# Squares and norm sums of chunk 5's K issued ahead of chunk 2's first layer (delta-rule attention followed by a GELU feed-forward layer)

## The chip, the cores and the metric

One core of one Trainium2 chip runs the whole program. The metric is the device time of one execution in microseconds (us). Before the change it is 646.0 us, the median of three runs (645.03 to 646.12).

## The reference

Two blocks follow each other. The first is a delta-rule recurrence over 768 positions for 4 batches and 8 heads of width 48; the second is a two-layer feed-forward net with an exact GELU on 3072 tokens (width 384, inner width 2048). Everything is float32.

```python
k_n = k / (np.linalg.norm(k, axis=-1, keepdims=True) + 1e-06)
for t in range(S):
    y[:, :, t] = einsum('bhd,bhde->bhe', q[:, :, t], state)
    v_old = einsum('bhde,bhd->bhe', state, k_n[:, :, t])
    state = state + bt * einsum('bhd,bhe->bhde', k_n[:, :, t], v[:, :, t] - v_old)
x = y.transpose(0, 2, 1, 3).reshape(B * S, H * D)
h = x @ w_in
out = (0.5 * h * (1.0 + erf(h / sqrt(2)))) @ w_out
```

## The kernel before, in words

The 768 positions are cut into 12 chunks of 64. A chunk has two units (`tiles[c, a]`, a = 0, 1), each holding two batches on the 128 partitions. For a chunk the recurrence is solved in closed form: a matrix of products of the chunk's keys with each other (`grams`, L414/L425), scaled by beta over the squared norm of each key, is inverted by forward elimination (`eliminate_steps`, L475 to L517), and with the inverse come the updates (`solve`), the outputs (`use`) and the new state. The two chunks of a pair (2g and 2g+1) share one elimination: its 30 steps run on VectorE on all the pair's units at once. Then the chunk's output goes through the feed-forward net: its first layer (`part_of_layer`, matmuls at L916) in two halves of 11 products each, by a scheme that saves multiplications and adds sums on VectorE; its second layer (`second_layer`, matmuls at L859) in seven products.

The step the change moves is the preparation of the key norms of chunk 5. It has two parts:

- `norms(5)` (L335 to L345, through `squares`, L309 to L320): for each of the two units one ScalarE activation, Square, of the unit's key tile `Kn` (128x384) into a tile `ksq`. The tile comes from the pool tag "x", which has two buffers; the same two serve the units' output tiles `x` (written by VectorE at L758, read by the transposes at L788 or L779 that turn a chunk's output). The activations go through `keep`, whose helper line is L902.
- `prep(5)` (L347 to L351): for each unit one VectorE sum over the row (L349, 128x384 to 128x8) into a part of the tile `n`, and one GpSimd power (L351, exponent 0.5) on the 128x16 elements of `n` for both units together.

What follows from them is `finish(4)`: `factors` (L303, L305, L306, L307 on VectorE) turns the norms of chunks 4 and 5, one tile, into the scale `gm` of the pair, and the elimination's first step (`scales`, L476 and L477, then `flip`, L482, and `scaled_flip`, L487) consumes it. `n` of chunk 4 alone is also used by `scale_v` (L376 on GpSimd).

`Kn` of chunks 4 and up is loaded (L100, SyncE's queue) into two tiles Kp[2] and Kp[3] that all these chunks share: chunk 6's load can be issued only when chunk 5's squares have read the tiles.

The order of the work is a plan: a list of (time, step) pairs, sorted by time and then issued. The times are in units of a chunk's feed-forward stage: the layer products of chunk c lie between c + 1 and c + 2 for c >= 2, so chunk 2's first layer begins at 3.0. VectorE's queue keeps exactly this order. On ScalarE the steps made with `keep` keep their order among themselves; other instructions of ScalarE, and all of TensorE's, SyncE's and GpSimd's, are ordered by the scheduler that builds the program from the dependencies. The plan around the place of the change, as (time, step), is:

- 2.851 to 2.922: the last parts of chunk 2's attention: `outputs` (L748, L758) and `turns` (transposes, and the ScalarE copies `xT<-psX`, here at L780)
- 2.955: `turned_k` of chunk 5 (L399), 2.958: `mix_x` (L884, four sums of x), 2.96: `last_sum_of_w` (L846)
- 3.0 on: chunk 2's first layer, products P1, P5, P6, P2, R22, R11, P7, P3, R12, P4, R21. P6 has a VectorE sum behind it (L939, in place in PSUM tile psY, with `pu`), P7 another (L947, psY and `pu` into G), and P4 writes psY again, so it can start only when L947 has read psY. R12 is followed by L958.
- 3.06: `add_p5` (L968), and `norms(5)`, `prep(5)`
- 3.07: `sum_of_w(4)` (L842, 128x1536)
- 3.11: `finish(4)`; 3.112: `scales`; 3.16 on: `flip` and the elimination, in pieces up to 4.2.

In time order, the VectorE queue of that stretch reads L399, L884 (four), L846, L939, L968, L349 (two), L842, L303, L305, L306, L307, L476, L477, L947, L482, L487, L958, L496 and the elimination.

Of the kernel before, what the change touches and what calls it, by code (L numbers as in the profile page):

```python
# [19 lines left out]
def kernel(  # L20
# [617 lines left out]
    def join_steps(g):  # L638
        a, b = range(NA), range(NA, 2 * NA)
        return [(join_run, g, a, ()), (join_run, g, b, a), (join_run, g, (), b)]  # L640
# [413 lines left out]
    def at(first, last, steps):  # L1054

        total, done, timed = sum(s[0] for s in steps), 0.0, []
        for w, *step in steps:
            timed.append((first + (last - first) * (done + 0.5 * w) / total, step))
            done += w
        return timed  # L1060
# [128 lines left out]
    def state_at(c, *times, first=(), second=()):  # L1189

        steps = state_steps(c, first, second)
        if len(times) > len(steps):
            steps = steps[:-1] + [(turn, tiles[c, a]) for a in range(NA)]
        return [(t, step) for t, step in zip(times, steps) if t is not None]
# [45 lines left out]
    def gram(c):  # L1240
        return [(grams, [tiles[c, a] for a in range(NA)])] if c < NC else []

    def query(c):
        return [(queries, [tiles[c, a] for a in range(NA)])]

    def spread(name, n, *times):
        return [at(t, t + 0.001, [(1.0, copy_out, name, n)]) for t in times]

    def rows_of(g, w, pieces):
        rows = eliminate_steps(g)  # L1250
        assert sum(n for n, _, _ in pieces) == len(rows)
        parts, done = [], 0
        for n, first, last in pieces:
            parts += [at(w + first, w + last, rows[done:done + n])]
            done += n
        return parts
# [8 lines left out]
    for w in range(3, NC):  # L1265
        two_ahead = w + 2 < NC
        if w % 2:
            if w == 3:
                plan += [at(w + 0.19, w + 0.191, [(1.0, transposed, u, (1,)) for u in fourth]),
                         at(w + 0.1, w + 0.101, [(1.0, together, *gram(5))]),  # L1270
                         at(w + 0.06, w + 0.061, [(1.0, norms, 5), (1.0, prep, 5)]),
                         at(w + 0.11, w + 0.111, [(1.0, finish, 4)])]
                plan += rows_of(2, w, ((1, 0.112, 0.113), (2, 0.16, 0.2), (4, 0.224, 0.31),
                                       (2, 0.325, 0.365), (1, 0.395, 0.4), (2, 0.485, 0.5),
                                       (2, 0.508, 0.54), (5, 0.6, 0.685), (7, 0.76, 0.88),
                                       (3, 1.0, 1.05), (5, 1.07, 1.1), (1, 1.153, 1.154),
                                       (1, 1.2, 1.201), (1, 1.201, 1.202)))
            elif two_ahead:
                plan += rows_of(w // 2 + 1, w, ((1, -0.35, -0.349), (1, -0.34, -0.339),
                                                (1, -0.23, -0.229), (5, -0.22, -0.14),  # L1280
                                                (1, -0.07, -0.06), (3, 0.005, 0.05),
                                                (3, 0.068, 0.148), (2, 0.156, 0.215),
                                                (2, 0.235, 0.31), (3, 0.325, 0.365),
                                                (1, 0.398, 0.409), (2, 0.485, 0.5),
                                                (1, 0.508, 0.54), (5, 0.6, 0.685),
                                                (3, 0.76, 0.8), (1, 1.003, 1.004),
                                                (1, 1.16, 1.161), (1, 1.166, 1.167)))
            plan += [state_at(w, w + 0.367, w + 0.59, w + 0.72, w + 0.93, second=query(w))]
        else:
            j0, j1, j2 = join_steps(w // 2)  # L1290
            t = w + (0.25 if w == 4 else 0.165)
            plan += [at(t, t + 0.001, [(1.0, together, j0, *query(w))]),
                     at(w + 0.37, w + 0.371, [(1.0, together, j1, *gram(w + 2))]),
                     state_at(w, w + 0.465, w + 0.58, w + 0.72, w + 0.93, second=[j2] + gram(w + 3))]
            plan += spread("join", 4, w + 0.395)
            plan += spread("join", 4, w + 0.64)
            if two_ahead:
                plan += spread("gram", 2, w + 0.375) + spread("gram", 2, w + 0.42)
                plan += spread("gram", 4, w + 0.63)
                plan += [at(w + 0.366, w + 0.367, [(1.0, norms, w + 2)]), at(w + 0.3715, w + 0.372, [(1.0, prep, w + 2)]),  # L1300
                         at(w + 0.56, w + 0.561, [(1.0, norms, w + 3), (1.0, prep, w + 3)]),
                         at(w + 0.64, w + 0.641, [(1.0, finish, w + 2)])]
# [32 lines left out]
```

## Time and profile before

One profiled execution took 644.96 us by the clock of the device; the profile's span is 643.2 us, so 1.76 us lie around it.

| What | Value |
|---|---|
| median of three runs | 646.0 us |
| lowest, highest | 645.03, 646.12 us |
| the profiled execution | 644.96 us |
| its span | 643.2 us |
| TensorE matmul busy | 617.9 us (96%) |
| VectorE busy | 496.3 us (77%) |
| ScalarE busy | 259.9 us (40%) |
| GpSimd busy | 66.0 us (10%) |
| mean granted TensorE clock | 0.985 |
| TensorE matmuls | 9702 |

A profile here has several views. The page gives the busy share of each engine in 40 slices of the span (one slice is 16.08 us), each digit a tenth, and a row PEclk with the clock granted to TensorE in the same digits. The list of waits adds up, for each engine and line, how long the engine sat idle before instructions of that line and what released it. A timeline lists instructions in order: start in us from the span's start, total duration in us, engine, line, operation, output<-input, how many instructions are merged, and in brackets the idle time before them with its releaser. A table of windows gives the busy time of each engine in a stretch, with the granted clock. PE is TensorE, DVE VectorE, ACT ScalarE, POOL GpSimd, SP SyncE; L12 is line 12 of the kernel.

### The profile page before, as it was taken

Reading aid. Unit: us, or ns where it says so; the run is one execution under the profiler, and the core shown is the slowest. Engines: PE = TensorE matmul, PEld = TensorE weight load, DVE = VectorE, ACT = ScalarE, POOL = GpSimd, SP = SyncE. Lnnn points to the kernel's source line nnn. Section 1 sums busy time; section 2 is a strip of 40 time slices with the busy share of each in tenths; the row PEclk is TensorE's granted clock in tenths of the full one; section 3 lists DMA queues with packets and bytes.
Section 4 is the critical chain, followed back from the end, with each engine's and each line's share of the span. In section 5 each row is a group of like instructions: output and inputs, shape, how many; then the busy total and the mean of one; then the engine's idle time right before and its main releaser. Section 6 shows DMA issues by size and latency. Waiting matters only on the chain.

```text
span 643.2 us, 22156 instructions
## 1 busy us (share of the span) xinstructions
PE 617.9 (96%) x9702; PEld 573.8 (89%) x9702; DVE 496.3 (77%) x1011; ACT 259.9 (40%) x586; POOL 66.0 (10%) x58
## 2 busy tenths in 40 slices
PE   6759999999989999999999999999999999999997
PEld 5658876776879999999999999999999999999997
DVE  6999989989589997999577999577999565354342
ACT  4576767524632256132266132266132253132230
POOL 4044002001301003001003001013001000000000
PEclk9987999999989999999999999999999999999999
DMA  9794683204422335312325312411211400100100
GB/s 135 174 273 159 129 199 113 45 1 74 84 37 42 56 43 91 58 24 37 66 34 86 61 21 41 67 21 33 51 25 35 69 3 3 25 2 3 25 2 24
DMA packets 158433, 39.79 MB, mean 62 GB/s; under 512 B 150016, under 2 KB 153216, under 8 KB 158336
## 3 DMA queue, kind: packets, MB, share of 16 engines
q1 hardware_dynamic: 155664, 37.34, 30.0%
q10 hardware_dynamic: 2672, 1.03, 0.8%
q8 instruction: 76, 1.25, 0.8%
q14 instruction: 21, 0.17, 0.1%
HBM read 33.62 MB, written 4.72 MB: 60 GB/s over the span
## 4 chain that ended last, share of the span: by engine, by line
PE 77%; DVE 14%; DMA 2%; issue 2%; SPq 2%; ACT 1%; POOL 1%; DVEq 0%; POOLq 0%
PE psX L859 12%; PE psY L916 11%; PE psY L859 8%; PE psX L916 8%; PE psV L916 5%; PE psZ L916 5%; PE psZ L859 4%; PE psV L859 4%; PE psK L667 3%; DVE Nu L503 3%; DVE tmp L501 3%; PE psG L414 3%; PE psJ L593 3%; PE psH L811 2%; PE psY L732 2%
## 5 line engine op out<-in xcount | busy, mean ns | idle before, releaser
L916 PE MATMUL psX<-xT,w_in_sb 128*128 128x128 f32 x480 | 64.8, 278 | 0.0
L503 DVE TENSOR_TENSOR Nu<-Nu,tmp 128x58 f32<-128x58 f32 (+13 forms) x168 | 57.9, 344 | 5.8
L501 DVE TENSOR_TENSOR tmp<-Nu 128x58 f32<-128x58 f32 (+13 forms) x168 | 58.0, 345 | 4.4
L916 PEld LDWEIGHTS psX<-xT,w_in_sb 128*128 128x128 f32 x480 | 59.4, 193 | 0.9
L902 ACT COPY xT<-psX 128x768 f32<-128x768 f32 x9 | 7.2, 799 | 124.3 <-PE psX L788 124.3
L351 POOL TENSOR_TENSOR n<-n,half 128x16 f32<-128x16 f32 x10 | 31.4, 3145 | 251.8 <-DVE n L349 191.2
L859 PE MATMUL psX<-w_out_sb,G 128*128 128x192 f32 x320 | 55.3, 326 | 0.0
L859 PEld LDWEIGHTS psX<-w_out_sb,G 128*128 128x128 f32 x320 | 52.1, 190 | 0.0
L811 PE MATMUL psH<-xT,w_in_sb 128*128 128x256 f32 x192 | 45.2, 390 | 0.5 <-ACT G L902 0.4
L829 PE MATMUL psO<-w_out_sb,G 128*128 128x384 f32 x128 | 43.9, 490 | 0.0
L811 PEld LDWEIGHTS psH<-xT,w_in_sb 128*128 128x128 f32 x192 | 36.3, 193 | 8.0 <-ACT G L902 1.3
L916 PE MATMUL psY<-xT,w_in_sb 128*128 128x128 f32 x320 | 43.1, 279 | 0.0
L916 PEld LDWEIGHTS psY<-xT,w_in_sb 128*128 128x128 f32 x320 | 39.8, 196 | 0.0
L902 ACT COPY pu<-psZ 128x512 f32<-128x512 f32 x40 | 23.5, 587 | 39.3 <-PE psZ L916 37.7
L829 PEld LDWEIGHTS psO<-w_out_sb,G 128*128 128x128 f32 x128 | 23.6, 190 | 14.0
L902 ACT ACTIVATE G<-G 128x512 f32<-128x512 f32 x40 | 25.2, 630 | 23.3 <-DVE G L947 22.6
L939 DVE TENSOR_TENSOR psY<-psY,pu 128x512 f32<-128x512 f32 x20 | 14.0, 698 | 22.4 <-PE psY L916 19.6
L376 POOL TENSOR_TENSOR V<-V,n 128x384 f32<-128x384 f32 x18 | 17.0, 959 | 135.4 <-DMA V<-in_v_dram 115.5
L859 PE MATMUL psZ<-T,pu 128*128 128x192 f32 x160 | 28.6, 332 | 0.0
L859 PE MATMUL psY<-T,G 128*128 128x192 f32 x160 | 28.6, 332 | 0.0
L859 PE MATMUL psV<-w_out_sb,G 128*128 128x192 f32 x160 | 27.7, 326 | 0.0
L859 PE MATMUL psX<-T,G 128*128 128x192 f32 x160 | 27.6, 326 | 0.0
(183 smaller groups left out, 1346.1 us busy)
## 6 DMA issues: line engine op xcount, KB each, us to landing
Kp<-in_k_dram SPq DMA_DIRECT2D x76, 96.0 KB, 3.2
w_out_sb<-in_moe_w_in_dram SPq DMA_DIRECT2D x24, 256.0 KB, 4.1
w_raw<-in_moe_w_out_dram SPq DMA_DIRECT2D x16, 384.0 KB, 4.5
V<-in_v_dram SPq DMA_DIRECT2D x48, 96.0 KB, 3.1
out_dram<-o_sb SPq DMA_DIRECT2D x40, 96.0 KB, 2.2
Qp<-in_q_dram SPq DMA_DIRECT2D x64, 32.0 KB, 2.1
Qp<-in_q_dram SPq DMA_DIRECT2D x16, 96.0 KB, 4.7
Qp<-in_k_dram SPq DMA_DIRECT2D x32, 32.0 KB, 2.2
```

Of the source, the lines that this page charges most:

```text
L351: nc.gpsimd.tensor_tensor(flat, flat, half, op=ALU.pow)
L376: engine.tensor_tensor(u.V, u.V, ns[u.c][:, u.a].unsqueeze(2).to_broadcast([128, H, D]), op=ALU.mult)
L414: nc.tensor.matmul(psG[HALF[p], r, i * NP + j, :], lhsT=u.Kt[rows, p, j, :], rhs=(u.Qt if x else u.Kt)[rows, p, j, :], start=True, stop=True)
L501: nc.vector.tensor_tensor(tmp, nu[:, j + 1:, j:j + 1].to_broadcast([128, n, j]), nu[:, j:j + 1, 0:j].to_broadcast([128, n, j]), op=ALU.mult)
L503: nc.vector.tensor_tensor(nu[:, j + 1:, 0:j], nu[:, j + 1:, 0:j], tmp, op=ALU.add)
L593: nc.tensor.matmul(psJ[HALF[p], k, :], lhsT=(xm if level else off)[rows, us, :], rhs=zf[rows, us, HB:C] if level else xm[rows, us, :], sta ...
L667: nc.tensor.matmul(u.psK[to, x, r, j, :], lhsT=(u.Qt if x else u.Kt)[rows, p, j, :], rhs=St[rows, u.a, p ^ r, j, :], start=True, stop=True)
L811: nc.tensor.matmul(psH, lhsT=w_in_sb[:, f // 2, m, f % 2 * 128:(f % 2 + 1) * 128], rhs=xTs[c][:, m, :], start=(m == 0), stop=(m == NM - 1))
L829: nc.tensor.matmul(u.psO, lhsT=G[:, u.a, f, :], rhs=w_out_sb[:, f, :], start=(f == 0), stop=(f == NF - 1))
L859: nc.tensor.matmul(ps_, lhsT=lhs[:, f, :], rhs=rhs[:, f, :], start=first and f == 0, stop=f == FH - 1, skip_group_check=not first)
L902: i = fn(*args, **kw)
L916: nc.tensor.matmul(ps_[:, i], lhsT=lhs[:, f // 2, f % 2 * 128:(f % 2 + 1) * 128], rhs=rhs, start=first and i == 0, stop=True, skip_group_c ...
```

## The change

In the plan for w = 3, `norms(5)` moves from time 3.06 to 2.93 and `prep(5)` from 3.0605 to 2.961. Nothing else in the source is touched.

```diff
             if w == 3:
                 plan += [at(w + 0.19, w + 0.191, [(1.0, transposed, u, (1,)) for u in fourth]),
                          at(w + 0.1, w + 0.101, [(1.0, together, *gram(5))]),
-                         at(w + 0.06, w + 0.061, [(1.0, norms, 5), (1.0, prep, 5)]),
+                         at(w - 0.07, w - 0.069, [(1.0, norms, 5)]), at(w - 0.039, w - 0.038, [(1.0, prep, 5)]),
                          at(w + 0.11, w + 0.111, [(1.0, finish, 4)])]
```

In the built program the two Square activations on ScalarE stand behind the second copy `xT<-psX` (L780) and ahead of the copy `o_sb<-psO` (L833); before, they stood between the two groups of copies out of the gram tiles (L425). The two sums L349 on VectorE stand ahead of L939 and L968; before, behind them. The GpSimd queue and TensorE's are unchanged in order. Two small shifts come along: on ScalarE the GELU that follows L947 now stands ahead of both copies of chunk 3's turned queries (L394; before, between them), and on SyncE's queue the four loads of chunk 6's `Kn` stand ahead of one piece of a `Kb` load (L138) instead of behind it.

## The prediction

> **What bounds the kernel now.** I read the page's slices first: where TensorE is full and where its clock falls.
>
> ```profile
> PE   6759999999989999999999999999999999999997
> ...
> PEclk9987999999989999999999999999999999999999
> ```
>
> From slice 3 on TensorE is full, except in slice 11 (176.9 to 193 us): 8 in busy time and 8 in clock. The list of waits for 150 to 196 us says what it waited for there:
>
> ```profile
> PE psY L916 <- DVE G L947: 4.0, 1, 4.0
> DVE n L303 <- POOL n L351: 2.8, 1, 2.8
> ```
>
> One wait of 4.0 us: product P4, which writes psY again, waited for the sum L947 that reads it; and VectorE, two steps upstream, waited 2.8 us for the GpSimd power. VectorE's timeline shows why L947 was late (columns: start, duration):
>
> ```profile
> 168.60 0.70 DVE L939 TENSOR_TENSOR psY<-psY,pu 128x512 f32<-128x512 f32 x1 [2.77 <-ACT diag L425]
> 169.40 0.69 DVE L968 TENSOR_TENSOR pu<-psY,pu 128x512 f32<-128x512 f32 x1
> 170.40 1.01 DVE L349 TENSOR_REDUCE n<-ksq 128x8 f32<-128x384 f32 x2 [0.30 <-ACT ksq L902]
> 171.33 1.75 DVE L842 TENSOR_TENSOR T<-w_out_sb,T 128x1536 f32<-128x1536 f32 x1
> 175.87 0.18 DVE L303 TENSOR_SCALAR n<-n 128x32 f32<-128x32 f32 x1 [2.79 <-POOL n L351]
> ...
> 179.27 0.68 DVE L947 TENSOR_TENSOR G<-psY,pu 128x512 f32<-128x512 f32 x1
> ```
>
> L947 stands behind the six instructions of `finish(4)` and `scales` (L303 to L477), which wait for the norms. Its own data were long there: P7 ended at 173.35, the copy of pu at 173.63. The source of the chain is on ScalarE and GpSimd:
>
> ```profile
> 162.62 0.48 ACT L780 COPY xT<-psX 128x384 f32<-128x384 f32 x1 [0.64 <-PE psX L779]
> 164.56 0.48 ACT L833 COPY o_sb<-psO 128x384 f32<-128x384 f32 x1 [1.46 <-PE psO L829]
> ...
> 169.84 0.94 ACT L902 ACTIVATE ksq<-Kp 128x384 f32<-128x384 f32 x2
> ```
>
> ```profile
> 171.49 4.35 POOL L351 TENSOR_TENSOR n<-n,half 128x16 f32<-128x16 f32 x1 [10.76 <-DMA Kp<-in_k_dram]
> ```
>
> The bracket on the last line names a load, but in the program this power waits for VectorE only (the sums ended at 171.41); the load merely landed nearby. The table of windows prices the stall's second half, the clock after it:
>
> ```profile
> 176.00:180.00 4.00, 0.01 (x1) 0.00 (x0) 3.83 (x8) 0.01 (x1) 1.61 (x2) 1.00 0.38 46
> 180.00:185.00 5.00, 4.99 (x30) 4.99 (x31) 4.79 (x9) 2.02 (x4) 0.00 (x0) 0.66 0.32 38
> 185.00:190.00 5.00, 5.00 (x157) 4.88 (x155) 3.59 (x9) 2.06 (x5) 0.00 (x0) 1.00 0.02 5
> ```
>
> The column after POOL's is the granted clock: 0.66 for the five us after the gap, else 1.00. For the rest of the span, up to its last product, the list of waits names no other wait of TensorE, so what it gains here reaches the end, unless VectorE gives it back.
>
> **What the Trainium skill says.** "TensorE: Matmul & The Clock Gate", Part 1: the clock falls to half after an idle window of about 3.4 us and returns after about as long of sustained work. The trace agrees: a 4.0 us gap, then 0.65 (180 to 182), 0.50 (182 to 184), 0.99 (184 to 186). "GPSIMD Engine Reference", section 1, says the SBUF interfaces are shared with VectorE, with contention from instructions with two SBUF inputs. It agrees: of ten powers nine took 2.90 us, and the one that took 4.35 ran under L842, a sum of two SBUF tiles. "ScalarE: Activation LUTs", "What ACT_TABLE_LOAD costs", prices a switch of function set at 2.66 us; the squares stood between copies and took 0.94 us with no gap, and copies stand around them again, so I add none.
>
> **The change part by part.** Profiled times, in us.
>
> *Squares, 0.94 on ScalarE.* They move behind the copy `xT<-psX`, which ends at 163.10, and end at 164.04. The next copy, `o_sb`, waits for TensorE until 164.56 anyway. The cover is that idle 1.46; without it the copies of the first layer would slip by at most 0.94. Two conditions. The data: chunk 5's K is issued from 149.59 to 153.52 and lands in about 3.0 (at most 4.0), by 157.5. The buffers "x": chunk 2's turns read them last, at 162.6, before the copy ahead in the same queue. At the old place ScalarE gets 0.94 back, ahead of chunk 5's gram copies; nothing late waits for them. Zero.
>
> *Sums, 1.01 on VectorE.* They follow L846 (164.08, 1.75, end 165.83) and end about 166.8. VectorE then stood idle until 168.60 (2.77 idle), because P6's product ends only there; L939 does not move. Zero; with the cover gone at most 0.93, and P7 (172.29) would still not wait for L939's end at 169.3.
>
> *Power, 2.90 to 4.35 on GpSimd.* It starts about 166.85, between two SBUF-heavy sums, and ends at 169.75; with contention at 171.2. I take 2.90, though both are hidden: VectorE comes to L303 later than either.
>
> *What VectorE then does.* L968 at 169.40; the next start comes 0.61 after it (as at 187.28 to 187.89), so L842 at 170.01, end 171.76, L303 at 171.77 instead of 175.87: 4.10 earlier. Of these 2.8 are the wait on GpSimd, 1.3 the sums and their wait no longer in front of L842. L303 to L947 takes 3.40, so L947 starts at 175.17 and ends at 175.87.
>
> *TensorE.* P4 comes 0.06 after L947's end: 175.93, where TensorE's work ahead runs out at 175.84 to 176.0. So 180.01 minus 175.93 = 4.08 earlier, and no idle window. With it goes the cold clock: P4, R21 and the next P1 took 4.41 (180.01 to 184.42); at 0.893 for eight matmuls, as everywhere later, 2.68. That is 1.73 more. Sum 5.81.
>
> *What is late next.* VectorE is 4.10 ahead, TensorE 5.81: VectorE must catch up from idle time. It has 0.93 before L939 at 186.48 and 0.38 before L678 at 190.25, both on TensorE. With P6 ending at 180.5 and VectorE ready at 181.44, the first goes (lead 5.01); the second goes too (lead 5.39). Then VectorE has no gap until 237.09. So it falls 0.42 behind. Where it was more than 0.42 ahead of its reader nothing happens: L947 at 192.27 ends 0.8 before P4 at 193.77; chunk 3's outputs end 4.9 before the turns. The tight place is the start of chunk 3's first layer: the reads of the second layer's PSUM tiles (L1013 to L1018, end 218.40 to 219.31) and the sum T1 (L884, end 219.52) against products at 218.85 and 219.74. Slack 0.1 to 0.45, so TensorE loses 0 to 0.4 there: I take 0.3, far too short for the clock. After 237 VectorE has room. 5.81 minus 0.3 = 5.5.
>
> *Small moves.* The GELU after L947 now holds ScalarE's two copies of chunk 3's queries (L394) until about 176.5; they end by 177.7, and their readers (psK, 188.09 before, about 182.3 after) are not near. Chunk 6's four loads of K pass one Kb piece on SyncE: that piece slips about 2.7 us, and its reader runs at 242.56. `norms` and `prep` issue no DMA themselves. Zero.
>
> Against the profiled 644.96: 639.5. That execution lies 1.04 below the median and 0.07 below the lowest run; against the median of 646.0: **640.5**.
>
> **The rivals.**
> *The stall goes, but less is gained.* VectorE's queue is full from 180 to 237, and if its two gaps don't close, TensorE is held to VectorE's lead of 4.1: 641.9. The same comes out if another short gap leaves the clock cold. For it: VectorE busy 9 tenths in slices 12 to 14. Against: both gaps are waits on TensorE itself.
> *Nothing changes.* If the power's lateness is only the last of several, L947 keeps its place: 646. For it: L482 and the rest are queued together. Against: 2.79 of idle time ends with that power alone.
> *Slower: the squares block ScalarE's queue.* They now stand ahead of `o_sb`, both copies `pu` and chunk 4's gram copies. If K of chunk 5 landed late, at t, all of these would follow: `o_sb` and `pu` (1.1), L939, L968, L842 (3.1), then 3.4 to L947. It decides from squares ending at about 171.6, that is K landing after 170.7; each us beyond costs one, and 2 us late would give 648. Against: it lands by 157.5, 13 us of margin.
>
> **How the numbers follow.** Main case 0.76; less gained 0.17; no change 0.03; slower 0.02; the last 0.02 lies below the range. Main case alone: 5.2 to 5.9 less than 645.03 to 646.12, with no loss at chunk 3 at the far end. The range reaches from 645.03 minus 5.9 = 639.1 to 646.1 minus 4.1 = 642.0. About 0.2% (1.3 us) is what a measurement can tell from no change. Faster 0.95, same 0.03, slower 0.02.
>
> **What would show it.** ksq on ScalarE near 163.1; L349 near 165.8; the power near 166.9 and 2.9 long; L303 near 171.8 with no wait on GpSimd; P4 near 176 with at most 0.2 us of wait; clock 1.00 from 180 to 185; a short wait of TensorE on VectorE near 213, at chunk 3's first layer. Wrong would be: the squares held after 164.5, L303 still waiting, or the clock cold despite the closed gap.

## The result and the profile after

The changed kernel takes 640.36 us (median of three runs, 639.25 to 640.82) against 646.0: a ratio of 0.9908, 95% interval 0.9892 to 0.9924. Measured once more, beside other runs on one chip, it was 0.9909 (0.9894 to 0.9923; 639.86 against 646.06). The profiled execution took 640.36, with a span of 638.7.

On the page, slice 11 has lost its dip in busy time and clock:

```profile
PE   6779999999999999999999999999999999999997
...
PEclk9977999999999999999999999999999999999999
```

VectorE's timeline of the changed kernel (start, duration; idle time in brackets):

```profile
166.48 1.00 DVE L349 TENSOR_REDUCE n<-ksq 128x8 f32<-128x384 f32 x2
169.33 0.70 DVE L939 TENSOR_TENSOR psY<-psY,pu 128x512 f32<-128x512 f32 x1 [1.85 <-ACT diag L425]
170.13 0.69 DVE L968 TENSOR_TENSOR pu<-psY,pu 128x512 f32<-128x512 f32 x1
170.74 1.75 DVE L842 TENSOR_TENSOR T<-w_out_sb,T 128x1536 f32<-128x1536 f32 x1
172.41 0.17 DVE L303 TENSOR_SCALAR n<-n 128x32 f32<-128x32 f32 x1
...
175.80 0.68 DVE L947 TENSOR_TENSOR G<-psY,pu 128x512 f32<-128x512 f32 x1
```

The sums stand in idle time ahead of L939, and L303 has no bracket: nothing was waited for. This profile ran 0.73 late from before the place of the change (L939 at 169.33 against 168.60; it needs TensorE's P6 in both). I therefore compare starts minus the start of this L939 in the same profile. ScalarE and GpSimd, the source of the chain:

```profile
163.36 0.48 ACT L780 COPY xT<-psX 128x384 f32<-128x384 f32 x1 [0.64 <-PE psX L779]
163.73 0.94 ACT L902 ACTIVATE ksq<-Kp 128x384 f32<-128x384 f32 x2
165.29 0.48 ACT L833 COPY o_sb<-psO 128x384 f32<-128x384 f32 x1 [0.62 <-PE psO L829]
```

```profile
167.56 2.90 POOL L351 TENSOR_TENSOR n<-n,half 128x16 f32<-128x16 f32 x1 [6.09 <-DVE n L349]
```

The squares used up part of ScalarE's idle time before `o_sb` (0.62 of 1.46 is left); the power took 2.90 and ended at 170.46, 1.95 before L303. TensorE and the windows:

```profile
175.68 1.06 PE L916 MATMUL psV<-xT,w_in_sb 128*128 128x128 f32 x8
176.58 1.12 PE L916 MATMUL psY<-TX,w_in_sb 128*128 128x128 f32 x8
177.54 1.06 PE L916 MATMUL psY<-xT,w_in_sb 128*128 128x128 f32 x8
```

```profile
176.00:180.00 4.00, 4.00 (x38) 4.00 (x37) 3.96 (x4) 2.61 (x5) 0.00 (x0) 1.00 0.48 70
180.00:185.00 5.00, 5.00 (x156) 4.83 (x154) 4.59 (x15) 1.87 (x4) 0.00 (x0) 1.00 0.42 52
```

P4 (second line) follows R12 after 0.90, the usual distance of two groups of eight; the clock column is 1.00 throughout. Starts after L939, in us, from the timelines:

| Marker on TensorE | before | after | earlier by |
|---|---|---|---|
| P4 of chunk 2, first half | 11.41 | 7.25 | 4.16 |
| P6 of the second half | 16.71 | 10.89 | 5.82 |
| P2 of chunk 3's first layer | 52.93 | 47.52 | 5.41 |
| last product of the program | 467.77 | 462.45 | 5.32 |

### The profile page after: what moved, and what is told of

Read it like the earlier page. It is cut to its first block, busy times and chain, and to the rows that moved or that the text cites. A ratio compares the mean times of both kernels' runs of the same rounds, so it can differ in the third digit from the quotient of the medians.

```text
span 638.7 us, 22156 instructions
## 1 busy us (share of the span) xinstructions
PE 618.4 (97%) x9702; PEld 573.8 (90%) x9702; DVE 496.6 (78%) x1011; ACT 259.9 (41%) x586; POOL 64.9 (10%) x58
## 3 DMA queue, kind: packets, MB, share of 16 engines
q10 hardware_dynamic: 2672, 1.03, 0.8%
## 4 chain that ended last, share of the span: by engine, by line
PE 81%; DVE 11%; ACT 2%; DMA 2%; issue 2%; POOL 0%; SPq 0%; DVEq 0%; ACTq 0%; POOLq 0%
PE psX L859 12%; PE psY L916 11%; PE psX L916 8%; PE psY L859 8%; PE psV L916 5%; PE psZ L916 5%; PE psG L414 5%; PE psZ L859 4%; PE psV L859 4%; PE psK L667 3%; PE psO L829 3%; PE psJ L593 2%; DVE tmp L501 2%; DVE Nu L503 2%; PE psH L811 2%; PE psY L732 2%
## 5 line engine op out<-in xcount | busy, mean ns | idle before, releaser
L376 POOL TENSOR_TENSOR V<-V,n 128x384 f32<-128x384 f32 x18 | 17.2, 965 | 135.3 <-DMA V<-in_v_dram 131.1
L939 DVE TENSOR_TENSOR psY<-psY,pu 128x512 f32<-128x512 f32 x20 | 14.0, 699 | 20.5 <-PE psY L916 18.7
```

The lines of the kernel that those rows point to most:

```text
L376: engine.tensor_tensor(u.V, u.V, ns[u.c][:, u.a].unsqueeze(2).to_broadcast([128, H, D]), op=ALU.mult)
L939: nc.vector.tensor_tensor(L1["Y1"], L1["Y1"], L1["pu"][:, 0], op=ALU.add)
```

## The experiments

My theory: the gain is the wait of TensorE before P4 (about 4.1) and the cold clock after it (1.7), less what VectorE can't follow (0.3). It hangs on one thing, that the norms are ready when VectorE comes to L303. Rivals: the gain came from clearing ScalarE's queue; the slow products after the wait are no clock effect or hidden; earlier is simply better. The summary first; ratios are against the kernel before, the two middle columns are starts after L939 in each profile.

| Run | P4 | P6, second half | ratio (95% interval) |
|---|---|---|---|
| before | 11.41 | 16.71 | 1 |
| after, second measurement | 7.25 | 10.88 | 0.9909 (0.9894 to 0.9923) |
| e1 squares only | 11.02 | 17.39 | 0.9994 (0.9984 to 1.0004) |
| e2 L842 early | 9.97 | 15.27 | 0.9961 (0.9950 to 0.9971) |
| e3 one power more | 8.29 | 11.97 | 0.9927 (0.9912 to 0.9942) |
| e4 two powers more | 11.16 | 16.25 | 0.9994 (0.9983 to 1.0005) |
| e6 norms earlier | 7.25 | 10.89 | 0.9905 (0.9890 to 0.9919) |
| e7 wait filled, 7.1 us of matmuls | 14.39 | 17.97 | 1.0012 (1.0003 to 1.0020) |
| e8 wait filled, 3.7 us of matmuls | 11.40 | 15.08 | 0.9970 (0.9958 to 0.9982) |
| e10 squares and L842 early | 9.57 | 13.24 | 0.9960 (0.9946 to 0.9974) |
| e11 power and a quarter more | 10.09 | 15.12 | 0.9964 (0.9950 to 0.9977) |

**Which part of the move counts: the squares alone.**

```diff
-at(w + 0.06, w + 0.061, [(1.0, norms, 5), (1.0, prep, 5)]),
+at(w - 0.07, w - 0.069, [(1.0, norms, 5)]), at(w + 0.0605, w + 0.061, [(1.0, prep, 5)]),
```

> Only the two squares move (2.93); the sums and the power stay at 3.0605. My theory (the end of the power decides, and VectorE's order decides when it starts): the sums begin right after L968, 0.4 earlier than before; the power runs under L842 again and takes 4.35; L303 comes about 0.4 earlier; TensorE still waits about 3.6 before P4. If the clock goes cold all the same, 0.4 faster than before (ratio 0.999); if 3.6 is short enough to keep it warm, 2.1 faster (0.997). Rival (the gain came from clearing ScalarE's queue of the squares): nearly the whole 5.6, ratio 0.991.

Measured: P4 0.39 earlier, ratio 0.9994. The rival is out: ScalarE's queue was cleared exactly as in the changed kernel, and the times show no gain that can be told from none. The profile of this run:

```profile
170.78 1.75 DVE L842 TENSOR_TENSOR T<-w_out_sb,T 128x1536 f32<-128x1536 f32 x1
175.32 0.18 DVE L303 TENSOR_SCALAR n<-n 128x32 f32<-128x32 f32 x1 [2.79 <-POOL n L351]
```

```profile
170.95 4.35 POOL L351 TENSOR_TENSOR n<-n,half 128x16 f32<-128x16 f32 x1 [10.36 <-DVE n L349]
```

The sums come 0.4 earlier, but the power again starts under L842, takes 4.35, and VectorE waits 2.79 for it as before. P6 of the second half even comes 0.68 later than before, because the clock stayed low for longer after the wait; the section on the wait and the clock returns to this.

**Is it the readiness of the norms: making them late again in the changed kernel.** One or two more powers of the same size are put ahead of chunk 5's in GpSimd's queue; the four other queues keep their order.

```diff
-        nc.gpsimd.tensor_tensor(flat, flat, half, op=ALU.pow)
+        [nc.gpsimd.tensor_tensor(wk.tile([128, NA * H], F32, tag=f"late{i}", name="late", bufs=1),
+          flat, half, op=ALU.pow) for i in range(1 if c == 5 else 0)]
+        nc.gpsimd.tensor_tensor(flat, flat, half, op=ALU.pow)
```

> The changed kernel with one more GpSimd power of the same size ahead of chunk 5's, into a tile that nothing reads. My theory: the real power ends 2.9 later than in the changed kernel, 4.35 later if it meets L842; it had 1.9 to spare before L303. So L303 slips by 1.0 to 2.4, TensorE waits about that long before P4, the clock stays at 1.00, and the time is 1.0 to 2.4 over the changed kernel, still 3.2 to 4.6 below the kernel before (ratio 0.993 to 0.995). Rival (any wait of TensorE cools the clock): 1.7 more, 2.7 to 4.1 over the changed kernel.

The profile with one more, TensorE's timeline and then VectorE's:

```profile
178.10 1.16 PE L916 MATMUL psY<-TX,w_in_sb 128*128 128x128 f32 x8 [0.88 <-DVE G L947]
179.10 1.06 PE L916 MATMUL psY<-xT,w_in_sb 128*128 128x128 f32 x8
```

```profile
173.96 0.18 DVE L303 TENSOR_SCALAR n<-n 128x32 f32<-128x32 f32 x1 [0.99 <-POOL n L351]
```

L303 waits 0.99, P4 comes 1.04 later than in the changed kernel and P6 1.08: a wait of 0.88 costs itself and no clock. The ratio lies 0.0018 to 0.0019 over the changed kernel's two, which is 1.2 us.

> The changed kernel with two more such powers ahead of chunk 5's, into tiles that nothing reads. My theory: the real power ends 5.8 to 7.2 later, so L303 slips by 3.9 to 5.3; TensorE waits that long before P4, which is over the idle time that cooled the clock in the kernel before, and loses another 1.7 at the cold clock. 5.6 to 7.0 over the changed kernel: between the kernel before and 1.4 slower than it (ratio 1.000 to 1.002). Rival (the gain doesn't hang on when the norms are ready): it stays as fast as the changed kernel, ratio 0.991.

Two more (the same edit with 2) bring the old time back: ratio 0.9994. The wait before P4 is 3.74, and P4 to P6 takes 5.09 instead of 3.64, so 1.45 go to the clock. My upper end was too high, because the last power was not stretched by L842 (below). So the whole gain can be taken away on GpSimd alone.

**Earlier still.** Norms at 2.84 and prep at 2.85, ahead of chunk 2's state update.

```diff
-at(w - 0.07, w - 0.069, [(1.0, norms, 5)]), at(w - 0.039, w - 0.038, [(1.0, prep, 5)]),
+at(w - 0.16, w - 0.159, [(1.0, norms, 5)]), at(w - 0.15, w - 0.149, [(1.0, prep, 5)]),
```

> The changed kernel with norms and prep of chunk 5 moved earlier still, to 2.84 and 2.85, ahead of chunk 2's state update and outputs on VectorE. My theory (it only matters that the norms are ready before VectorE comes to L303; there were 1.9 to spare): the same time as the changed kernel, within 0.5. The squares now wait on ScalarE for chunk 4's sums to free their buffers and for chunk 5's K, until about 157.8, with nothing due behind them; VectorE waits about 1.5 for the sums before L748, and chunk 2's turns come at most 0.3 late. Rival (earlier is better): more gain. Rival (a place that blocks VectorE's queue costs what it blocks): 1.5 slower than the changed kernel.

The two markers of the table agree with the changed kernel's to 0.01, the last product to 0.05; the ratio is 0.9905. Both powers now run back to back from 158.73 and end eight us before they are read; it brings nothing. Being ready is enough.

**The clock by itself.** In the kernel before, TensorE's wait is filled with matmuls that nothing reads.

```diff
+            [behind(nc.tensor.matmul, t, block(1, 1)[:, 0, 0:128], of_x(c, 2, 0), True, True)
+             for t in ([dn("warm")[:, 0, 0:128]] * 32 if (c, b) == (2, 0) else [])]
             product(L1["Y1"], block(1, 1), L1["T"][4], False)
```

> The kernel before, with 32 matmuls (128x128 each, into a PSUM tile that nothing reads) put on TensorE between R12 and P4, where it waits for L947. They take 3.6 of the 4.0, so P4 starts where it did. My theory (the second part of the gain is the cold clock): the clock stays at 1.00 from 180 to 185, P4, R21 and P1 take 2.7 instead of 4.4, and the kernel is 1.7 faster than before although it does more work and waits as long: 644.2, ratio 0.9973. Rival (the slow products after the wait come from something else, or their slowness is hidden): 646, no change.

I had mis-sized it. One such matmul counts as two pieces of 0.11, so 32 took 7.1 us and P4 came 2.98 later than before. Even so P6 came only 1.26 later and the time rose by 0.0012 (0.8 us): 1.72 came back at a warm clock. With half as many:

> The kernel before with 16 instead of 32 matmuls (128x128, read by nothing) between R12 and P4: the profile of the 32 showed 64 pieces and 7.1 us, so 16 take 3.6, which fit into the wait of 4.0. My theory (the second part of the gain is the cold clock): clock 1.00 after the gap, P4 starts where it did, and the eight-matmul groups after it take 0.89 from the first on; 1.7 faster than before, 644.3, ratio 0.9973. Rival (the slow groups are something else than the idle time's clock): 646, no change.

Measured 0.9970, 644.20 against 645.91. The timeline of TensorE and the windows of this run:

```profile
175.55 3.74 PE L892 MATMUL warm<-xT,w_in_sb 128*128 128x128 f32 x32
179.71 1.16 PE L916 MATMUL psY<-TX,w_in_sb 128*128 128x128 f32 x8 [0.42 <-DVE G L947]
180.71 1.06 PE L916 MATMUL psY<-xT,w_in_sb 128*128 128x128 f32 x8
```

```profile
178.00:180.00 2.00, 1.58 (x14) 1.39 (x13) 2.00 (x3) 0.31 (x1) 0.00 (x0) 1.00 0.43 50
180.00:182.00 2.00, 2.00 (x20) 2.00 (x20) 1.97 (x2) 1.00 (x3) 0.00 (x0) 1.00 0.43 52
```

P4 starts where it did in the kernel before (11.40 against 11.41), the clock stays at 1.00, and P6 comes 1.63 earlier. The kernel does more and waits for the same sum, and is 1.7 us faster: the cold clock is the second part of the gain, shown apart from the first. The seven executions lie within 0.7 us of each other, those of the kernel before on the same chip within 3.0, which fits a loss to the clock that differs from one execution to the next.

**The contention between the power and L842.** The kernel before with L842 in VectorE's idle time.

```diff
-at(3.07, 3.071, [(1.0, sum_of_w, 4)])
+at(2.962, 2.963, [(1.0, sum_of_w, 4)])
```

> The kernel before, with L842 (the sum of second-layer weights, 128x1536) moved from 3.07 to 2.962, into VectorE's idle time ahead of L939. Norms stay late. My theory: the power no longer runs under a sum of two SBUF tiles and takes 2.90 instead of 4.35, so L303 and L947 come about 1.5 earlier and TensorE waits about 2.5 instead of 4.0. If the cold clock needs an idle time of more than about 3.4, it stays warm and the gain is 1.5 + 1.7 = 3.2 (ratio 0.995); if any wait of some us brings it, the gain is 1.5 (0.9977). Rival (the power is slow for another reason, its place in time or the loads in flight): 4.35 again, no gain.

```profile
172.75 2.90 POOL L351 TENSOR_TENSOR n<-n,half 128x16 f32<-128x16 f32 x1 [10.76 <-DMA Kp<-in_k_dram]
```

```profile
179.82 1.16 PE L916 MATMUL psY<-TX,w_in_sb 128*128 128x128 f32 x8 [2.56 <-DVE G L947]
180.82 1.47 PE L916 MATMUL psY<-xT,w_in_sb 128*128 128x128 f32 x8
182.07 1.92 PE L916 MATMUL psX<-xT,w_in_sb 128*128 128x128 f32 x8
```

The power takes 2.90, P4 comes 1.44 earlier. But in this profile the wait of 2.56 is followed by slow groups (1.47, 1.92 where 1.06 is normal): P4 to P6 takes 5.30, as in the kernel before. So the limit of 3.4 us that the prediction had taken over failed here. The ratio, 0.9961 or 2.5 us, lies between the two values I had named, and its sixteen executions show why: eight took 642.61 to 642.94, about 3.3 below the kernel before, which is the value for a warm clock; the other eight, the profiled one among them, took 643.58 to 645.86.

**How long a wait cools the clock.** Both edits e1 and e2 at once, and the changed kernel with one power and a small one more (16 and 4 columns).

> The kernel before with both the squares at 2.93 and L842 at 2.962; the sums and the power stay at 3.0605. My theory: the sums follow L968 at once, the power takes 2.90 with nothing under it, L303 comes 1.9 earlier than before, and TensorE waits about 2.1. The wait of 2.56 in the run with L842 early still cooled the clock and one of 0.88 didn't; if 2.1 is enough for it, the gain is 1.9 (ratio 0.997), if not, 1.9 + 1.7 = 3.6 (0.9944).

> The changed kernel with two more GpSimd powers ahead of chunk 5's, one of 16 columns and one of 4, into tiles that nothing reads. If the time of a power goes with its columns, the small one takes about 0.7 and TensorE waits about 1.6 before P4; if it is the same for any size, 2.9 and 3.8. With 1.6 and a warm clock, 1.6 over the changed kernel (ratio 0.9935); with 1.6 and a cold one, 3.3 over it (0.996); with 3.8, as with two full powers (0.9994).

```diff
+        [nc.gpsimd.tensor_tensor(wk.tile([128, w], F32, tag=f"late{w}", name="late", bufs=1),
+          flat[:, 0:w], half[:, 0:w], op=ALU.pow) for w in ((16, 4) if c == 5 else ())]
         nc.gpsimd.tensor_tensor(flat, flat, half, op=ALU.pow)
```

P4 of the first run, then of the second:

```profile
178.36 1.16 PE L916 MATMUL psY<-TX,w_in_sb 128*128 128x128 f32 x8 [2.16 <-DVE G L947]
179.35 1.06 PE L916 MATMUL psY<-xT,w_in_sb 128*128 128x128 f32 x8
```

```profile
179.81 2.08 PE L916 MATMUL psY<-TX,w_in_sb 128*128 128x128 f32 x8 [2.68 <-DVE G L947]
181.67 1.55 PE L916 MATMUL psY<-xT,w_in_sb 128*128 128x128 f32 x8
```

After 2.16 the groups are at full speed (P4 to P6 3.67), after 2.68 not (5.03). The ratio of e10, 0.9960 or 2.6 us, lies between my two values, and its eight executions fall into two groups: three at 642.10 to 642.59, the profiled one among them, and five at 643.75 to 644.33. The groups lie 1.7 apart, the size of the clock's loss. So I read that a wait of about 2.2, like that of 2.56 in e2, cools the clock in some executions and not in others; the five were not profiled, so this is not shown directly.

In e11 the small power took 1.01 where I had expected 0.7. The real power started only 0.5 later than in e3, but that was 0.32 behind the start of L842, and it was stretched to 4.19; so the wait was 2.68 and not 1.6.

What decides it can be read from the clock column in narrow windows. e2, where the clock fell after P4 had started:

```profile
180.00:182.00 2.00, 2.00 (x16) 2.00 (x17) 1.97 (x2) 1.39 (x3) 0.00 (x0) 0.82 0.40 49
182.00:184.00 2.00, 2.00 (x12) 2.00 (x11) 1.93 (x5) 0.60 (x1) 0.00 (x0) 0.50 0.39 45
184.00:186.00 2.00, 2.00 (x16) 2.00 (x16) 1.25 (x5) 1.26 (x3) 0.00 (x0) 0.82 0.25 30
```

In windows of 0.25 us the clock is either 1.00 or 0.50, except at the two ends. So a mean of 0.82 over 2 us means 0.7 us at 0.50, and the clock was low from about 181.3 to 184.7. The same reading of all the profiles with a longer wait:

| Profile | TensorE waits | clock at 0.50 | half of that after P4's start | measured loss, P4 to P6 |
|---|---|---|---|---|
| before | 176.01 to 180.01 | 180.61 to 184.02 | 1.71 | 1.66 |
| e1 | 175.87 to 179.47 | 178.33 to 185.15 | 2.84 | 2.73 |
| e4 | 176.29 to 180.03 | 179.61 to 183.02 | 1.50 | 1.45 |
| e2 | 177.26 to 179.82 | 181.30 to 184.71 | 1.71 | 1.66 |
| e11 | 177.13 to 179.81 | 179.28 to 182.70 | 1.44 | 1.39 |
| e10 | 176.20 to 178.36 | never | 0 | 0.03 |

The low stretch lasts 3.41 us, once twice that, and what it costs is half of the part that falls on work. Its ends are not tied to the wait: in a profile the changes of the clock lie whole multiples of 3.413 apart (before: up at 57.73 near the program's start, down at 180.61, 36 multiples later, up again one later). If each profile is cut into stretches of that length, TensorE was idle for 1.9 us or more (1.9 to 3.3) in the stretch that ended with each of the five falls, and for at most 1.5 in every stretch around the wait after which the clock stayed up. In e10 a boundary, counted on from the clock's changes near the start, fell into the wait and left 1.5 before it and 0.6 behind. That is a reading of these profiles, not a run of its own; it explains why the same wait can cost 1.7 in one execution and nothing in another.

**Where 0.4 to 0.5 of the gain went.** The changed kernel with VectorE's turns of chunk 4's queries moved out of the tight place at chunk 3's first layer.

```diff
-        t = c + (-0.12 if c % 2 == 0 else 0.23)
+        t = c + (0.16 if c == 4 else -0.12 if c % 2 == 0 else 0.23)
         plan += [at(t, t + 0.01, [(1.0, turned_q, u) for u in us])]
```

> The changed kernel with the two turns of chunk 4's queries on VectorE (L404, 1.23 together) moved from 3.88, ahead of the reads of the second layer's PSUM tiles, to 4.16, behind L512. My theory (what is lost between the gain of 5.8 at chunk 3's state products and 5.3 at the end is VectorE being late at chunk 3's first layer): the reads L1013 to L1018 and the sums L884 come 1.2 earlier against TensorE, the two short waits at that layer's first products go, and 0.3 to 0.5 more is gained: 640.0, or 0.4 below the changed kernel, best seen in the profile at those products. Rival (the rest was lost elsewhere, or is noise between runs): no change there, the same time.

In this kernel the load of chunk 5's queries comes ahead of the turns of chunk 4's, so chunk 4 computes with the wrong queries; the instructions and their sizes are the same. The time did not improve (0.9915, 0.9901 to 0.9930). The first products did come earlier (P2 of chunk 3 at 47.10 after L939 instead of 47.52), but the list of waits names a new one:

```profile
PE psY L916 <- ACT G L902: 0.9, 1, 0.9
```

The turns now delay L516, and ScalarE's copies L520, which wait for it, stood ahead of the GELU that frees psY. The second try mends both: the load of chunk 5's queries goes from 4.1 to 4.18, and the copies L520 from 4.201 to 4.26, so that they stand behind that GELU.

```diff
+        t = 3.2 if c == 4 else c - (0.72 if c % 2 == 0 else 0.82 if c == 5 else 0.9)
...
-                                       (1, 1.2, 1.201), (1, 1.201, 1.202)))
+                                       (1, 1.2, 1.201), (1, 1.260, 1.261)))
```

> The changed kernel with the turns of chunk 4's queries (L404) at 4.16 as before, the load of chunk 5's queries behind them, and the last elimination step (the copies L520 on ScalarE) moved from 4.201 to 4.26, so that the GELU of psY stands ahead of them. My theory: the 0.3 to 0.5 that TensorE lost at chunk 3's first layer stays won, since the wait of 0.9 for that GELU, which ate it in the first try, goes: 0.4 below the changed kernel, ratio 0.990, seen in the profile as no wait of TensorE and the second psX group of chunk 3's first layer 0.4 earlier. Rival: another wait takes its place, the same time as the changed kernel.

Chunk 3's first two products in the changed kernel, then in this one:

```profile
213.94 1.13 PE L916 MATMUL psX<-xT,w_in_sb 128*128 128x128 f32 x8
214.97 1.16 PE L916 MATMUL psZ<-TX,Sw 128*128 128x128 f32 x8
```

```profile
213.21 1.05 PE L916 MATMUL psX<-xT,w_in_sb 128*128 128x128 f32 x8
214.10 1.06 PE L916 MATMUL psZ<-TX,Sw 128*128 128x128 f32 x8
```

The distance of the two is 1.03 in the first and 0.89, the usual, in the second. P2 stands at 47.11, the last product at 461.96 against 462.45: 0.5 us more, which shows where VectorE's lateness reached TensorE. (In e10's profile the first of these products waits 0.15 for L1013 by name.) It is the fastest kernel here, 639.32 us (639.19 to 639.50), ratio 0.9894 (0.9879 to 0.9910), but the intervals overlap with the changed kernel's: that it is faster is shown by the profile's markers, not by the times.

Why VectorE was late there shows further up. Compared as before by starts after L939, it is ahead of the kernel before by 5.18 at the second half's L939 and by 5.82 at L684 and L958, as far as TensorE; 3 us later, and from there on to chunk 3, by 5.33. In between, two of its short instructions were longer (they take 0.34 to 0.38 otherwise), each while GpSimd ran a product of V (L376):

```profile
189.66 0.83 POOL L376 TENSOR_TENSOR V<-V,n 128x384 f32<-128x384 f32 x1 [15.32 <-DMA V<-in_v_dram]
190.89 0.87 POOL L376 TENSOR_TENSOR V<-V,n 128x384 f32<-128x384 f32 x1 [0.41 <-DMA V<-in_v_dram]
```

```profile
189.83 0.86 DVE L501 TENSOR_TENSOR tmp<-Nu 128x184 f32<-128x184 f32 x1
191.11 0.87 DVE L501 TENSOR_TENSOR tmp<-Nu 128x198 f32<-128x198 f32 x1
```

In the kernel before only one was:

```profile
196.11 0.88 DVE L503 TENSOR_TENSOR Nu<-Nu,tmp 128x198 f32<-128x198 f32 x1
```

One such instruction more is the 0.5. The profiles of the second measurement and of e3, e5, e6, e9 and e10 have two as well. No run moved L376, so that it could be won back there is not shown.

## Why the prediction was right

640.5 was forecast, 640.36 measured, and the main steps hold one by one: the wait before P4 goes, and the cold clock with it. That the median came within 0.14 is luck: the changed kernel's executions lie up to 1.6 us apart, and the second measurement gives a gain of 6.2 where the first gives 5.6.

- *Squares, sums, power.* All three stood where the working put them, within 0.1 once the 0.73 is taken off, and hid behind the covers named. The squares alone moved P4 by 0.39 (e1).
- *L303 and P4.* 4.10 was forecast for L303; it came at 3.08 after L939 instead of 7.27, so 4.19. P4: forecast 4.08, measured 4.16.
- *The clock.* 1.73 forecast, 1.66 measured between P4 and P6, and 1.7 in a run of its own (e8). The price was read from one execution, and that it fits the median is partly luck: e1's profile lost 2.73 after a shorter wait.
- *VectorE late at chunk 3.* The place was right, the reason wasn't. 0.3 was forecast out of 0 to 0.4; 0.41 was measured between P6 and P2, and another 0.1 by the end. It surfaced where the prediction said and was won back there by moving 1.2 us of VectorE work (e9). But VectorE was to be 0.42 behind because its idle time would not suffice to catch up. It caught up fully, to 5.82, and then lost 0.49 to GpSimd's products of V, which the prediction doesn't name. That the two come to about the same is luck.
- *The slower rival.* The squares found their data in time: 0.62 of idle time was left before `o_sb`. A late load of K was not tried.

Two more reasons were less right than the number. I took over the limit of the Trainium skill, "TensorE: Matmul & The Clock Gate", Part 1, an idle window of about 3.4 us, and wrote that the trace agrees; 4.0 couldn't test it. The length of 3.4 us does come back here, as that of the low stretches. But waits of 2.56 and 2.68 cooled the clock in the profiled executions, 0.88 and 2.16 didn't, and by the spread of the executions 2.2 and 2.56 do it in some and not in others. The measurement decides. For this change it made no difference, since the wait goes altogether; for half the change it would have.

The other is the stretched power. The Trainium skill, "GPSIMD Engine Reference", section 1, names contention with VectorE instructions that have two SBUF inputs, and I read "ran under L842". The count behind it was also wrong: of the ten powers seven took 2.90, one 2.94, one 3.85 (the first, at 51.42) and the one in question 4.35. In e3 the real power ran from 171.02 to 173.92, almost wholly under L842 (171.22 to 172.97), and took 2.90. What counts is the start:

```profile
171.02 2.90 POOL L351 TENSOR_TENSOR n<-n,half 128x16 f32<-128x16 f32 x1
```

It began 0.20 before L842. In the five profiles where it began 0.16 to 0.32 after L842's start it took 4.19 to 4.35, and ended 2.75 to 2.77 after L842's end each time. So it looks as if it waits for the running sum to finish and is not slowed by it. The first power of the program, which I didn't take apart, need not follow the same count.

## What to carry to other kernels

When a full engine waits once, walk back to the first instruction whose inputs were ready long before, and move that into idle time ahead; being ready in time is all that counts, and going earlier brings nothing. Price the wait with what the clock costs after it, here 1.4 to 2.7 us in the profiles where a wait of 2.6 us or more was followed by a low clock, and measure more than one execution, since the same wait may cost it or not. Then ask who falls behind once the wait is gone, and check it instruction by instruction: an engine that is nearly full gives each lost half microsecond back at its next tight place.

## What the runs showed of the hardware

- After waits of TensorE of 2.56 to 4.0 us five profiles have a clock of 0.50 for 3.41 us (6.83 in e1); after 0.88 and 2.16 there was none. The loss between P4 and P6 was 1.66 (wait 4.0), 2.73 (3.60), 1.45 (3.74), 1.66 (2.56) and 1.39 (2.68): it goes not with the wait but with how much of the low stretch falls on work.
- In five profiles a GpSimd power of 128x16 that started during a VectorE sum of two SBUF tiles ended 2.75 to 2.77 us after that sum, as if it had waited for it. The other way round, VectorE instructions of 0.36 us that started 0.17 to 0.22 us after a GpSimd product of 128x384 took 0.86 and 0.87 and ended about 0.2 after it. In e11 a power of four columns took 1.01, one of 16 took 2.90.
- An fp32 matmul of 128x128 shows as two pieces of 0.11 us each in this profile.
